# Decode attention and a Mish layer on one core: w2's seventh rows on partitions 0 to 63, last values in 3/4 and 1/4, o turned ahead of w2's products

## The chip, the cores and the metric

The kernel runs on one core of one Trainium2 chip. The time is device time in microseconds (us) of one execution. The kernel before was run three times: 1311.62, 1311.73 and 1311.91 us, median 1311.73. Only its own profile and trace were at hand when the prediction was written.

## What is computed

One decode step of a layer that adds attention over a long cache and a dense layer with Mish to its input. Cut to what matters:

```python
x: (8, 1, 512)                       # 8 sequences, one new token each
xn  = layernorm(x)
# A: attention, 32 query heads over 8 key heads, cache of 8192 positions, 128 per head
q   = (xn @ wq) by heads;  k, v = caches (8, 8, 8192, 128), each used by 4 query heads
p   = softmax(q . k * 128**-0.5);  o = p @ v;  A = o @ wo          # wo: (4096, 512)
# B: the dense layer
h   = xn @ w1 + b1                                                 # w1: (512, 1792)
act = h * tanh(softplus(h));       B = act @ w2                    # w2: (1792, 512)
return x + A + B
```

All is float32. The two caches hold 268 MB each, and every byte of them is read once.

## The kernel before

The caches are read as 64 blocks of 8 MB: for each of 16 packs p (a pair of key heads and two sequences b = 0, 1) one block of k and one of v per sequence, with 64 KB on each of the 128 partitions. Three buffers in SBUF take them in turn. `kva` ("a") takes w1, one block of k and then the blocks of v; `kvb` ("b") takes the blocks of k, at the end the block of v of the last pack's first sequence and after it w2; `kvw` ("w") takes wq and wo, 2 MB at a time.

All loads stand in one list (`queue`). `plan` (L114) appends one load per part; a part is a share of the columns of all 128 partitions. `pump` (L103) takes loads from the front while their buffer is free and issues them on SyncE (SP), and `release` (L110) gives a buffer up when the products that read it have been written down. On the chip SP waits for those products, by columns: a part's load is issued when PE has read the columns that it overwrites. The order of the loads is thus fixed, and SP is the only engine that issues them; ScalarE (ACT) issues two small ones at the start, x and b1. PE, VectorE (DVE) and GpSimd run in the order in which the code is written, which L710 to L727 make a rule.

The main loop (L651) computes for each pack the scores (`scores`, L348, products c on PE), the row maximum, exponents on ACT, their transposes and sums on DVE (`weights`, L423), and, one pack behind, the products with v (`values`, L454: 32 matmuls for a block, four column groups in each round, two trace records for a matmul). `gather` (L468) picks and adds the parts of a sequence's products (one DVE instruction and three more), `merge` (L484) sums them over partition groups with one matmul and scales them into `oT`. After the four packs of a pair of heads `turn` (L498) turns o so that it can be multiplied with wo: one DVE copy of the identity into `tid`, four matmuls, and four copies of 32 partitions into `oW`, for the last pair alternately on DVE and ACT.

`mish` (L567) runs once near the start: h for 1792 columns as four groups of 448 on four groups of partitions, some 14 DVE instructions, and a transpose into `aT`, the operand of w2's products. w2 lies in `kvb` as seven rows of 1024 numbers on each partition. `down(lo, hi)` (L620) multiplies rows lo to hi: 2 x 4 matmuls a row.

The end of the kernel (L687 to L708), in PE's order: the values of the last pack's first sequence (from `kvb`), its sums and merge, `add_up` (x and the earlier outputs), the values of the second sequence in two halves (from `kva`, loaded in two parts), w2's first four rows, the merge, the turn, half of wo's products, w2's fifth and sixth row, the other half of wo's, w2's seventh row. DVE copies the sum and SP stores it. The loads of this end, in SP's order:

```python
    plan_v(PACKS - 1, 0, "b")
    plan_v(PACKS - 1, 1, "a", ((0, 1 / 2), (1 / 2, 1)))
    W2_PARTS = ((0, 4), (4, 6), (6, 7))
    for k, (lo, hi) in enumerate(W2_PARTS):
        plan("w2", "b", w2, ((lo / W2R, hi / W2R),))
        if k < 2:
            plan_wo(PAIRS - 1, ((k / 2, (k + 1) / 2),))
```

Of the kernel before, what the change touches and what calls it, by code (L numbers as in the profile page):

```python
# [8 lines left out]
F32 = mybir.dt.float32  # L9
# [4 lines left out]
P = 128  # L14
B = 8
D = 512
# [49 lines left out]
OR = 4  # L66
W1R = 2 * CC * P // P
W2R = G * FT // 2 * FP // P
FAR = 1e38


@with_exitstack
def kernel(
# [40 lines left out]
    def plan(what, at, blocks, parts=((0, 1),), lo=0):  # L114

        rows = rows_of(blocks)
        n = rows.shape[1]
        t = place[at][:, lo : lo + n]

        def load(cols):  # L120
            nc.sync.dma_start(t[:, cols], rows[:, cols])
            return t

        for first, end in parts:
            cols = slice(int(first * n), int(end * n))
            queue.append((what, at, lambda cols=cols: load(cols)))


# [28 lines left out]
    def plan_wo(i, parts=((0, 1),)):  # L157
        plan(("wo", i), "w", wo[i * 4 : i * 4 + 4], parts)


    plan_wq(0)
    plan("w1", "a", w1)
# [10 lines left out]
            if p > 0:  # L173
                plan_v(p - 1, b, "a")
    plan_v(PACKS - 1, 0, "b")
    plan_v(PACKS - 1, 1, "a", ((0, 1 / 2), (1 / 2, 1)))
    W2_PARTS = ((0, 4), (4, 6), (6, 7))
    for k, (lo, hi) in enumerate(W2_PARTS):
        plan("w2", "b", w2, ((lo / W2R, hi / W2R),))
        if k < 2:  # L180
# [36 lines left out]


    xnT = const.tile([P, QR, 2, Q], F32, name="xnT")
    aT = const.tile([P, 2 * W2R, Q], F32, name="aT")  # L220
    xw = aT.rearrange("p j q -> p (j q)")[:, : W1R * 2 * B]
    xw = xw.rearrange("p (r t b) -> p r t b", r=W1R, t=2)

    def setup():
        make_identity(nc, ident)
        nc.gpsimd.memset(ones, 1.0)
        nc.vector.memset(xnT, 0.0)
        nc.vector.memset(H, 0.0)

        st = const.tile([B, 8], F32, name="st")  # L230

        scratch = pt.rearrange("p b c m t e h -> p (b c m t e h)")
        xc, sq = scratch[:B, :D], scratch[:B, D : 2 * D]
        nc.vector.reduce_sum(st[:, 0:1], x_sb, axis=AX.X)
        nc.vector.tensor_scalar_mul(st[:, 1:2], st[:, 0:1], 1.0 / D)
        nc.vector.tensor_scalar(xc, x_sb, st[:, 1:2], None, op0=ALU.subtract)
        nc.vector.tensor_mul(sq, xc, xc)
        nc.vector.reduce_sum(st[:, 2:3], sq, axis=AX.X)
        nc.vector.tensor_scalar(
            st[:, 3:4], st[:, 2:3], 1.0 / D, EPS, op0=ALU.mult, op1=ALU.add  # L240
        )
        nc.scalar.activation(st[:, 4:5], st[:, 3:4], AF.Sqrt)
        nc.vector.reciprocal(st[:, 5:6], st[:, 4:5])

        nc.vector.tensor_mul(st[:, 6:7], st[:, 5:6], st[:, 5:6])
        nc.vector.tensor_mul(st[:, 7:8], st[:, 6:7], st[:, 3:4])
        nc.vector.tensor_scalar(st[:, 6:7], st[:, 7:8], -0.5, 1.5, op0=ALU.mult, op1=ALU.add)
        nc.vector.tensor_mul(st[:, 4:5], st[:, 6:7], st[:, 5:6])
        nc.vector.tensor_scalar(xc, xc, st[:, 4:5], None, op0=ALU.mult)
        for r in range(QR):  # L250
            nc.tensor.transpose(M[:, r * B : (r + 1) * B], xc[:, r::QR], ident[:B, :B])
        nc.vector.tensor_copy(
            xnT[:, :, :, :B],
            M[:, : QR * B]
            .rearrange("p (r o b) -> p r o b", r=QR, o=1)
            .to_broadcast([P, QR, 2, B]),
        )
# [24 lines left out]
        nc.vector.memset(csel, 0.0)  # L282
        for c in range(2):
            rows = slice(HE * c, HE * (c + 1))
            for b in range(PB):
                nc.vector.tensor_copy(
                    csel[rows, b, :, b], ident[rows, rows].rearrange("p (u h) -> p u h", u=KN)
                )
        return wide
# [205 lines left out]
                RT.pop(p).rearrange("p b e h -> p (e h) b"),  # L495
            )

    def turn(i):  # L498


        to = oW[i] = work.tile([P, OR, 2, B], F32, name="oW")

        tid = work.tile([P, HT * KINDS * P], F32, name="e", bufs=1)[:, : OR * P]
        tid = tid.rearrange("p (r g i) -> p r g i", r=OR, g=G)
        nc.vector.tensor_copy(
            tid, ident.rearrange("p (i r o) -> p r o i", r=OR, o=1).to_broadcast([P, OR, G, Q])
        )
        o = oT.pop(i).rearrange("p n h b -> p (n h b)")
        cols = 2 * REP * B
        for r in range(OR):  # L510
            nc.tensor.matmul(
                M[:, 256 + r * cols : 256 + (r + 1) * cols],
                tid[:, r].rearrange("p g i -> p (g i)"),
                o,
                start=True,
                stop=True,
            )
        m = M[:, 256 : 256 + OR * cols].rearrange("p (r j q) -> p j r q", r=OR, j=G)
        for j in range(G):
            rows = slice(Q * j, Q * (j + 1))  # L520
            dst = to[rows].rearrange("p r h b -> p r (h b)")
            if i == PAIRS - 1 and j % 2:
                nc.scalar.copy(dst, m[rows, j])
            else:
                nc.vector.tensor_copy(dst, m[rows, j])
# [41 lines left out]
    def mish(w1_sb):  # L567


        hp = H[:, :FG]  # L570
        for g in range(G):
            nc.tensor.matmul(
                hp[Q * g : Q * g + B, :], gsel[:, g, :], b1_sb, start=True, stop=False
            )
        for r in range(W1R):
            for g in range(G):
                at = r * F // 2 + g % 2 * FG
                nc.tensor.matmul(  # L578
                    hp[Q * g : Q * g + B, :],
                    xw[:, r, g // 2, :],  # L580
                    w1_sb[:, at : at + FG],
                    start=False,
                    stop=(r == W1R - 1),
                )

        scratch = work.tile([P, HT * KINDS * P], F32, name="e", bufs=1)
        h, a, z, z2 = (scratch[:, i * 512 : i * 512 + FG] for i in range(4))
        nc.vector.tensor_copy(h, hp)


        nc.vector.scalar_tensor_tensor(a, h, -1.0, h, op0=ALU.mult, op1=ALU.max)
# [2 lines left out]
        m = a  # L594
        nc.vector.tensor_single_scalar(m, h, 0.0, op=ALU.is_gt)

        one = acc[:, :FG]
        nc.vector.tensor_scalar(one, z2, -1.0, 1.0, op0=ALU.mult, op1=ALU.add)
        nc.vector.tensor_mul(one, one, m)
        t1 = m  # L600
# [6 lines left out]
        nc.vector.tensor_mul(t1, t2, z)  # L607
        act = one
        half = FG // 2
        for e in range(2):  # L610
            nc.vector.tensor_mul(
                act.rearrange("p (i a e l) -> p e a l i", a=2, e=2, i=W2R)[:, e],
                h[:, half * e : half * (e + 1)].rearrange("p (a l i) -> p a l i", a=2, i=W2R),
                t1[:, half * e : half * (e + 1)].rearrange("p (a l i) -> p a l i", a=2, i=W2R),
            )
# [4 lines left out]
    def down(lo, hi, w):  # L620

        for j in range(2 * lo, 2 * hi):
            for g in range(G):
# [3 lines left out]
                    aT[:, j, :B],  # L627
                    w[:, at : at + P],
                    start=False,
                    stop=(j == 2 * W2R - 1),  # L630
                )


# [17 lines left out]
    for p in range(PACKS):  # L651
        for b in range(PB):
# [7 lines left out]
            if b == 0 and p > 0:  # L660
                sums(p - 1, lsel.pop(p - 1))
                if p > 1 and (p - 1) % NP == 0:
                    turn((p - 1) // NP - 1)
            rows(b)
            if b == 1:
                maximum(p)
# [19 lines left out]

    p = PACKS - 1  # L687
    merges()
    values(0, landed["v", p, 0])
    gather(p, 0)  # L690
    release(("v", p, 0))
    sums(p, lsel.pop(p))
    merge(p, 0)
    add_up()
    values(1, landed["v", p, 1], 0, ROUNDS // 2)
    values(1, landed["v", p, 1], ROUNDS // 2)
    gather(p, 1)
    w2_sb, wo_sb = landed["w2"], landed["wo", PAIRS - 1]
    down(*W2_PARTS[0], w2_sb)
    merge(p, 1)  # L700
    turn(PAIRS - 1)
    last_outputs(0, OR // 2, wo_sb)
    down(*W2_PARTS[1], w2_sb)
    last_outputs(OR // 2, OR, wo_sb)
# [61 lines left out]
```

## Time and profile before

| | us |
|---|---|
| median of three runs | 1311.73 |
| the profiled execution, its own time | 1311.59 |
| its span, first to last instruction | 1309.8 |
| DVE reads the finished sum, from the span's start | 1307.02 |
| PE busy in the span | 858.9 |
| DVE busy in the span | 384.7 |
| ACT busy in the span | 111.6 |

The profile is of one execution, and its times count from the start of the span; the 1.8 us that the execution's own time is longer lie around the span. A row of the chain of waits has the start, the length in us, and the engine and line or the transfer that the end of the kernel hung on. A row of the timeline has the start, the length, the engine, the line, the operation, output and input, and in brackets the idle time before it and what ended it. PEld is the load of a matmul's weights, which runs beside PE. A row of the DMA issues has the transfer, the issuing engine's queue (SPq, ACTq), how many, the size of each and the median time from issue to landing. Queue q1 is SP's, q10 is ACT's. A row of the windows has the window, its length, the busy time and records of each engine, the granted clock of PE as a share of full speed, the share of the 16 DMA engines that was busy, and GB/s.

### The profile page before, as it was taken

How to read it: one execution, taken by the hardware profiler on the slowest of the kernel's cores; microseconds unless marked ns; L12 is line 12 of the kernel's file. 1: busy time of each engine (PE TensorE's matmuls, PEld its weight loads, DVE VectorE, ACT ScalarE, POOL GpSimd, SP SyncE). 2: the span in 40 equal slices, each digit the busy share in tenths (PEclk: the TensorE clock that was granted, in tenths of full speed). 3: DMA queues.
4: the chain of work that ended last, by engine and by line, in shares of the span. 5: the costliest groups of instructions: out<-in, count | busy, mean ns of one | idle time of the engine just before them, and what ended most of it. 6: DMA issues, size and time to landing. Idle time of an engine off the chain costs nothing.

```text
span 1309.8 us, 10688 instructions
## 1 busy us (share of the span) xinstructions
PE 858.9 (66%) x4764; PEld 278.7 (21%) x4764; DVE 384.7 (29%) x590; ACT 111.6 (9%) x294; POOL 4.8 (0%) x10
## 2 busy tenths in 40 slices
PE   4786556856567765677566686665775666766567
PEld 1221112212112221122211222111221221222113
DVE  6150505205051230521405032052320505114051
ACT  1020101001010100101101010010100101011010
POOL 1000000000000000000000000000000000000000
PEclk9897889887799788898878897878987888878888
DMA  9999999999999999999999999999999999999997
GB/s 404 443 421 441 429 437 428 434 439 425 438 429 439 429 437 425 441 423 445 419 440 423 418 448 425 441 425 439 427 435 426 429 437 423 443 427 435 435 424 334
DMA packets 11446, 561.76 MB, mean 429 GB/s; under 512 B 1276, under 2 KB 1408, under 8 KB 1544
## 3 DMA queue, kind: packets, MB, share of 16 engines
q1 hardware_dynamic: 11376, 561.06, 99.3%
q8 instruction: 37, 0.61, 0.2%
q10 hardware_dynamic: 24, 0.02, 0.0%
q14 instruction: 9, 0.07, 0.0%
HBM read 561.01 MB, written 0.07 MB: 428 GB/s over the span
## 4 chain that ended last, share of the span: by engine, by line
DMA 60%; PE 35%; DVE 4%; issue 0%; ACT 0%; ACTq 0%; DVEq 0%
DMA kvb<-in_kT 56%; PE c L353 31%; DMA kva<-in_kT 2%; PE o L460 2%; DMA kvb<-in_w 2%; DVE raw L412 1%; DVE pt L430 1%; PE h L578 0%; PE h L312 0%; DVE nm L379 0%; PE s L365 0%; PE h L625 0%; DVE raw L421 0%; DVE os L473 0%; PE h L559 0%
## 5 line engine op out<-in xcount | busy, mean ns | idle before, releaser
L353 PE MATMUL c<-kvb,qT 128*64 128x512 f32 x1984 | 497.7, 665 | 348.4 <-DMA kvb<-in_kT 325.8
L353 PEld LDWEIGHTS c<-kvb,qT 128*64 128x64 f32 x1984 | 160.8, 154 | 685.3 <-issue 381.8
L460 PE MATMUL o<-kva,pt 128*32 128x512 f32 x1984 | 234.3, 626 | 25.5 <-DMA kva<-in_v 25.5
L379 DVE TENSOR_REDUCE nm<-s 128x1 f32<-128x1024 f32 x16 | 19.6, 1225 | 462.5 <-PE s L365 462.5
L412 DVE STREAM_TRANSPOSE raw<-e 128x2048 f32<-128x2048 f32 x32 | 116.0, 3627 | 14.4 <-ACT e L404 12.7
L360 ACT COPY sc<-c 128x512 f32<-128x512 f32 x32 | 18.7, 585 | 1001.3 <-PE c L353 1001.3
L460 PEld LDWEIGHTS o<-kva,pt 128*32 128x32 f32 x1984 | 64.5, 115 | 185.2 <-issue 144.1
L404 ACT ACTIVATE e<-s,nms 128x512 f32<-128x512 f32 x128 | 86.2, 685 | 126.2 <-DVE nms L393 66.8
L492 DVE TENSOR_TENSOR oT<-m,r 128x16 f32<-128x16 f32 x16 | 2.8, 175 | 233.6 <-PE m L488 233.6
L471 DVE TENSOR_SCALAR os<-o,isel 128x128 f32<-128x128 f32 x32 | 11.2, 350 | 152.0 <-PE o L460 152.0
L430 DVE TENSOR_TENSOR pt<-raw 64x256 f32<-64x256 f32 x128 | 53.6, 419 | 2.0
L365 PE MATMUL s<-sc,csel 64*128 64x512 f32 x128 | 36.1, 641 | 8.1 <-ACT sc L360 8.1
L421 DVE TENSOR_TENSOR raw<-raw 128x1024 f32<-128x1024 f32 x32 | 39.2, 1226 | 1.1
L340 DVE TENSOR_TENSOR qT<-qc,bsel 128x1024 f32<-128x1024 f32 x32 | 37.7, 1219 | 0.0
L473 DVE SCALAR_TENSOR_TENSOR os<-o,isel,os 128x128 f32<-128x128 f32 x96 | 33.7, 351 | 3.4
L404 ACT ACTIVATION_READ_ACCUMULATOR e<-s,nms 128x1 f32 x128 | 26.0, 203 | 0.0
L380 PE MATMUL m<-ident,nm 128*1 128x128 f32 x16 | 4.3, 270 | 21.2 <-DVE nm L379 21.2
L312 PE MATMUL h<-kvw,xnT 128*64 128x512 f32 x64 | 16.4, 660 | 0.0
L488 PEld LDWEIGHTS m<-hsel,os 128*128 128x128 f32 x64 | 9.5, 188 | 27.9 <-issue 23.7
L460 PE MATMUL o<-kvb,pt 128*32 128x512 f32 x64 | 9.5, 758 | 8.5 <-DVE oT L492 8.5
L353 PE MATMUL c<-kva,qT 128*64 128x512 f32 x64 | 14.0, 593 | 1.4 <-DMA kva<-in_kT 1.4
L323 DVE TENSOR_SCALAR e<-h 128x512 f32<-128x512 f32 x16 | 9.9, 683 | 16.1 <-PE h L312 16.1
(98 smaller groups left out, 170.8 us busy)
## 6 DMA issues: line engine op xcount, KB each, us to landing
kvw<-in_wq SPq DMA_DIRECT2D x4, 2048.0 KB, 31.1
kva<-in_v SPq DMA_DIRECT2D x2, 4096.0 KB, 23.5
kvw<-in_wo SPq DMA_DIRECT2D x3, 2048.0 KB, 30.4
kva<-in_w SPq DMA_DIRECT2D x1, 3584.0 KB, 16.0
kvb<-in_w SPq DMA_DIRECT2D x1, 2048.0 KB, 20.5
kvw<-in_wo SPq DMA_DIRECT2D x2, 1024.0 KB, 24.4
kvb<-in_w SPq DMA_DIRECT2D x1, 1024.0 KB, 24.1
kvb<-in_w SPq DMA_DIRECT2D x1, 512.0 KB, 26.9
```

The costliest lines, as they stand in the source:

```text
L312: nc.tensor.matmul(H[HE * e : HE * (e + 1), :], xnT[:, r].rearrange("p g q -> p (g q)"), w[:, r * BW + e * D : r * BW + (e + 1) * D], star ...
L340: nc.vector.tensor_mul(qT[:, b], qc[:, k * PB + b] .rearrange("p r (o h) -> p r o h", o=1) .to_broadcast([P, KR, KN, REP]), bsel.rearrange ...
L353: nc.tensor.matmul(C[b][HE * c : HE * (c + 1), :], t[:, r], k[:, r * BW + c * 512 : r * BW + (c + 1) * 512], start=(r == order[0]), stop=( ...
L360: nc.scalar.copy(sc, C[b])
L365: nc.tensor.matmul(S[:, c * 512 : (c + 1) * 512], csel[HE * c : HE * (c + 1), b].rearrange("p u b h -> p (u b h)"), sc[HE * c : HE * (c + ...
L379: nc.vector.tensor_reduce(nm, S, axis=AX.X, op=ALU.max, negate=True)
L404: nc.scalar.activation(ex[:, :, s, :], S[:, c * 512 : (c + 1) * 512].rearrange("p (t f) -> p t f", t=HT), AF.Exp, bias=NMS[p][:, s : s + 1 ...
L412: nc.vector.transpose(raw.rearrange("p (m t r) -> p t m r", m=TW, t=HT), ex.rearrange("p t s (q m) -> p t m (s q)", m=TW),)
L421: nc.vector.tensor_add(raw[:, :, :n], raw[:, :, :n], raw[:, :, n:])
L430: nc.vector.tensor_add(pt[rows, b, c].rearrange("p m t e h -> p (m t) e h")[:, :, e], raw[rows, :, at : at + REP], raw[rows, :, V8 + at : ...
L460: nc.tensor.matmul(O[b][Q * c : Q * (c + 1), :], pt[:, b, j % 2, j // 2].rearrange("p t e h -> p (t e h)"), vt[:, W4 * DH * j : W4 * DH * ...
L473: nc.vector.scalar_tensor_tensor(os, O[b][:, DH * i : DH * (i + 1)], isel[:, i : i + 1], os, op0=ALU.mult, op1=ALU.add,)
```

## The change

It has four parts, three of them at the end of the kernel.

- The load of w2's seventh rows. Before, it was the last load of SP's queue, 4 KB for each of 128 partitions. Now `plan_last_w2` issues it on ACT, ahead of the rest of w2 in the list: eight transfers, transfer k to the partitions k, k + 8, ... k + 56 of the first 64. Each of these partitions takes two rows, its own seventh and that of the partition 64 above it. On SP then stand w2's first four rows, half of wo, the fifth row, the other half of wo, the sixth row.
- `mish` computes the seventh rows' part of act a second time in the arrangement that this needs: 2 + 16 more matmuls of 64 columns into the PSUM buffer O[0], vectors of 512 columns for 448, one DVE copy, one DVE product and one memset more.
- The values of the last sequence are loaded and multiplied in 3/4 and 1/4. Between the two stands `last_down`, the 16 matmuls of the seventh rows, on 64 partitions.
- `turn` is split: the copy of the identity (`turning`) goes to the start of the end, and the merge and the turn stand ahead of `down` of the first four rows.

```diff
+    def plan_last_w2():
+        rows = w2.rearrange("j p f -> (j p) f").rearrange(
+            "(x e k i) f -> k i e x f", x=2, e=8, i=W2R
+        )
+        t = place["b"][:, (W2R - 1) * BW : W2X * BW].rearrange("p (x f) -> p x f", x=2)
+
+        def load():
+            for k in range(HE // 8):
+                nc.scalar.dma_start(t[k : HE : HE // 8], rows[k, W2R - 1])
+            return place["b"]
+
+        queue.append(("w2", "b", load))
...
-    plan_v(PACKS - 1, 1, "a", ((0, 1 / 2), (1 / 2, 1)))
-    W2_PARTS = ((0, 4), (4, 6), (6, 7))
+    plan_v(PACKS - 1, 1, "a", ((0, 3 / 4), (3 / 4, 1)))
+    plan_last_w2()
+    W2_PARTS = ((0, 4), (4, 5), (5, 6))
...
+        for g in range(2):
+                at = r * F // 2 + g * FG
+                nc.tensor.matmul(
+                    hx[Q * g : Q * g + B, :],
+                    xw[:, r, 1, :],
+                    w1_sb[:, at + W2R - 1 : at + FG : W2R],
...
+    def last_down(w):
+        for j in range(2 * W2R - 2, 2 * W2X):
+            for g in range(G):
+                at = j * D + g * P
+                nc.tensor.matmul(
+                    H[Q * g : Q * g + B, :P],
+                    aT[:HE, j, :B],
+                    w[:HE, at : at + P],
+                    start=False,
+                    stop=False,
+                )
...
     merges()
+    tid = turning()
     values(0, landed["v", p, 0])
...
     add_up()
-    values(1, landed["v", p, 1], 0, ROUNDS // 2)
-    values(1, landed["v", p, 1], ROUNDS // 2)
+    values(1, landed["v", p, 1], 0, ROUNDS * 3 // 4)
+    w2_sb, wo_sb = place["b"], landed["wo", PAIRS - 1]
+    last_down(w2_sb)
+    values(1, landed["v", p, 1], ROUNDS * 3 // 4)
     gather(p, 1)
-    w2_sb, wo_sb = landed["w2"], landed["wo", PAIRS - 1]
+    merge(p, 1)
+    turn(PAIRS - 1, tid)
     down(*W2_PARTS[0], w2_sb)
-    merge(p, 1)
-    turn(PAIRS - 1)
     last_outputs(0, OR // 2, wo_sb)
     down(*W2_PARTS[1], w2_sb)
     last_outputs(OR // 2, OR, wo_sb)
```

More of the change, by code (lines that the diff above doesn't have):

```diff
@@ L68 @@
 W2R = G * FT // 2 * FP // P
+W2X = W2R + 1
+XG = FG // W2R
 FAR = 1e38
@@ L124, in plan @@
         for first, end in parts:
-            cols = slice(int(first * n), int(end * n))
+            cols = slice(round(first * n), round(end * n))
             queue.append((what, at, lambda cols=cols: load(cols)))
@@ L219 @@
     xnT = const.tile([P, QR, 2, Q], F32, name="xnT")
-    aT = const.tile([P, 2 * W2R, Q], F32, name="aT")
+    aT = const.tile([P, 2 * W2X, Q], F32, name="aT")
     xw = aT.rearrange("p j q -> p (j q)")[:, : W1R * 2 * B]
@@ L228, in setup @@
         nc.vector.memset(H, 0.0)
+        nc.vector.memset(O[0][:, :XG], 0.0)
         st = const.tile([B, 8], F32, name="st")
@@ L496, in merge, with turning @@
             )
-    def turn(i):
-        to = oW[i] = work.tile([P, OR, 2, B], F32, name="oW")
+    def turning():
         tid = work.tile([P, HT * KINDS * P], F32, name="e", bufs=1)[:, : OR * P]
@@ L507, in turn @@
         )
+        return tid
+    def turn(i, tid):
+        to = oW[i] = work.tile([P, OR, 2, B], F32, name="oW")
         o = oT.pop(i).rearrange("p n h b -> p (n h b)")
@@ L570, in mish @@
         hp = H[:, :FG]
+        hx = O[0][:, :XG]
         for g in range(G):
@@ L573, in mish @@
                 hp[Q * g : Q * g + B, :], gsel[:, g, :], b1_sb, start=True, stop=False
+            )
+        for g in range(2):
+            nc.tensor.matmul(
+                hx[Q * g : Q * g + B, :],
+                gsel[:, 2 + g, :],
+                b1_sb[:, W2R - 1 :: W2R],
+                start=True,
+                stop=False,
             )
@@ L584, in mish @@
                 )
+            for g in range(2):
+                at = r * F // 2 + g * FG
+                nc.tensor.matmul(
+                    hx[Q * g : Q * g + B, :],
+                    xw[:, r, 1, :],
+                    w1_sb[:, at + W2R - 1 : at + FG : W2R],
+                    start=False,
+                    stop=(r == W1R - 1),
+                )
         scratch = work.tile([P, HT * KINDS * P], F32, name="e", bufs=1)
-        h, a, z, z2 = (scratch[:, i * 512 : i * 512 + FG] for i in range(4))
-        nc.vector.tensor_copy(h, hp)
+        n = FG + XG
+        h, a, z, z2 = (scratch[:, i * 512 : i * 512 + n] for i in range(4))
+        nc.vector.tensor_copy(h[:, :FG], hp)
+        nc.vector.tensor_copy(h[:, FG:], hx)
         nc.vector.scalar_tensor_tensor(a, h, -1.0, h, op0=ALU.mult, op1=ALU.max)
@@ L595, in mish @@
         nc.vector.tensor_single_scalar(m, h, 0.0, op=ALU.is_gt)
-        one = acc[:, :FG]
+        one = acc[:, :n]
         nc.vector.tensor_scalar(one, z2, -1.0, 1.0, op0=ALU.mult, op1=ALU.add)
@@ L609, in mish @@
         half = FG // 2
+        nc.vector.tensor_mul(
+            act[:, FG:].rearrange("p (a e l) -> p a e l", a=2, e=2),
+            h[:, FG:].rearrange("p (e a l) -> p a e l", a=2, e=2),
+            t1[:, FG:].rearrange("p (e a l) -> p a e l", a=2, e=2),
+        )
         for e in range(2):
             nc.vector.tensor_mul(
-                act.rearrange("p (i a e l) -> p e a l i", a=2, e=2, i=W2R)[:, e],
+                act[:, :FG].rearrange("p (i a e l) -> p e a l i", a=2, e=2, i=W2R)[:, e],
                 h[:, half * e : half * (e + 1)].rearrange("p (a l i) -> p a l i", a=2, i=W2R),
@@ L629, in down @@
                     start=False,
-                    stop=(j == 2 * W2R - 1),
+                    stop=(j == 2 * W2R - 3),
+                )
+    def last_down(w):
+        for j in range(2 * W2R - 2, 2 * W2X):
+            for g in range(G):
+                at = j * D + g * P
+                nc.tensor.matmul(
+                    H[Q * g : Q * g + B, :P],
+                    aT[:HE, j, :B],
+                    w[:HE, at : at + P],
+                    start=False,
+                    stop=False,
                 )
@@ L662 @@
                 if p > 1 and (p - 1) % NP == 0:
-                    turn((p - 1) // NP - 1)
+                    turn((p - 1) // NP - 1, turning())
             rows(b)
```

## The prediction, made before the changed kernel ran

> **What bounds the kernel now.** I read the page first, its engine shares and its queues, then the chain of waits and the instructions of the last 50 us, because every edit but one in the mish block lies there.
>
> ```profile
> span 1309.8 us, 10688 instructions
> DMA  9999999999999999999999999999999999999997
> q1 hardware_dynamic: 11376, 561.06, 99.3%
> q10 hardware_dynamic: 24, 0.02, 0.0%
> ```
>
> SP's queue (q1) keeps the DMA engines busy in every slice but the last: the kernel is a 561 MB stream, and only what happens while the stream ends can move the time by more than a fraction. The chain of waits over the end:
>
> ```profile
> 1272.95 3.67 PE o L460 x16
> 1276.64 20.51 DMA kvb<-in_w
> 1297.20 1.93 PE h L625 x64
> 1299.13 0.33 PE m L488 x2
> 1299.48 0.18 DVE oT L492
> 1299.66 0.53 DVE e L505
> 1300.23 1.12 PE m L511 x8
> 1301.38 0.22 DVE oW L525
> ...
> 1302.11 0.21 ACT oW L523
> 1302.37 1.90 PE h L559 x32
> 1304.27 1.37 PE h L625 x32
> 1305.63 0.87 PE h L559 x32
> 1306.51 0.49 PE h L625 x16
> 1307.02 0.29 DVE acc L707
> ```
>
> From 1297.20 on the end is set by computing: w2's first rows have landed, and PE, DVE and ACT pass o along one after the other until DVE reads the sum at 1307.02. But the stream is close behind. The last issues with their times to landing, and two windows of the end (columns: window, us, busy of PE, PEld, DVE, ACT, POOL, clock, DMA share, GB/s):
>
> ```profile
> kva<-in_v SPq DMA_DIRECT2D x2, 4096.0 KB, 23.5
> kvb<-in_w SPq DMA_DIRECT2D x1, 2048.0 KB, 20.5
> kvb<-in_w SPq DMA_DIRECT2D x1, 512.0 KB, 26.9
> 1259.08 3.76 SPq L121 DMA_DIRECT2D kva<-in_v  x2
> 1279.04 0.44 SPq L121 DMA_DIRECT2D kvb<-in_w  x1
> 1298.00:1301.50 3.50, 2.55 (x54) 2.10 (x42) 0.82 (x3) 0.00 (x0) 0.00 (x0) 1.00 0.98 407
> 1301.50:1305.40 3.90, 3.03 (x64) 2.28 (x68) 0.31 (x2) 0.41 (x2) 0.00 (x0) 0.56 0.44 181
> ```
>
> w2's last 512 KB land at 1279.04 + 26.9 = 1305.9, about 0.6 us ahead of their use at 1306.51. And the engines don't end together: at 0.98 until 1301.5, then 0.44 for 3.9 us. I read this as about half of the sixteen done near 1302 and the others some 2.6 us later (0.44 x 3.9 = 1.7 us of work that all sixteen could have shared).
>
> **The change, part by part.** *Mish.* 18 more matmuls, 36 records, and vectors of 512 columns for 448.
>
> ```profile
> 20.18 6.20 PE L578 MATMUL h<-kva,aT 128*8 128x448 f32 x64
> 26.44 0.33 SPq L121 DMA_DIRECT2D kva<-in_kT  x1
> 1.63 0.42 SPq L121 DMA_DIRECT2D kvb<-in_kT  x1
> kvb<-in_kT SPq DMA_DIRECT2D x1, 35.9
> ```
>
> At most 36 x 6.20/64 = 3.5 us on PE. What waits for it is SP's issue of the second k block at 26.44; the first one still moves until 1.63 + 35.9 = 37.5, so 11 us of stream cover it, less some 3 us for engines that end early. DVE's additions (a seventh more columns) come before the first maximum and hide behind the same stream. I take 0; without the cover it would be 3.5 us.
>
> *Last values.* The first piece grows from 4 to 6 MB.
>
> ```profile
> 1272.95 9.47 PE L460 MATMUL o<-kvb,pt 128*32 128x512 f32 x64 [8.47 <-DVE oT L492]
> 1284.84 5.23 PE L460 MATMUL o<-kva,pt 128*32 128x512 f32 x32
> 1292.30 3.64 PE L460 MATMUL o<-kva,pt 128*32 128x512 f32 x32 [2.23 <-DMA kva<-in_v]
> 1284.80:1288.20 3.40, 3.36 (x20) 0.92 (x24) 0.52 0.98 419
> 1296.01 0.35 DVE L471 TENSOR_SCALAR os<-o,isel 128x128 f32<-128x128 f32 x1 [11.84 <-PE o L460]
> 1296.40 1.12 DVE L473 SCALAR_TENSOR_TENSOR os<-o,isel,os 128x128 f32<-128x128 f32 x3
> ```
>
> The first half landed at 1259.08 + 23.5 = 1282.6, the second at 1292.3: 4 MB in 9.7 us, so three quarters land at 1287.4. Then 48 records: 20 in 3.4 us at the clock of 0.52 that the row shows after a lull, 28 at 3.64/32 = 0.114 us, 6.6 in all: PE is done at 1294.0. The last quarter is 1.82 us instead of 3.64. Shifted PE work ahead of the last landing saves nothing by itself, as PE was waiting there (2.23 us).
>
> *Turn.* The copy of the identity (0.53) leaves the chain for a place at 1272.8, where DVE's next step waits for the 9.47 us of values on kvb. The merge and turn no longer stand behind w2's 64 records, and the four copies of oW (1301.38 to 1302.33) hide behind those 1.93 us. Together about 1.5 us off the chain of computing, if PE can start it in time.
>
> *w2's seventh rows.* Removed: the row as last transfer of SP. Added: eight transfers on ACT's queue, each eight partitions of two 4 KB rows, issued when PE is through half of the values on kvb (32 records, 16 after w2's issue at 1276.64: about 1278.4). In PE's order their 16 matmuls stand between the third and the fourth quarter of the values and wait for all eight; behind them are queued the last quarter, the merge, the turn, everything to the end. So what matters is when they land. The trace has one transfer of this kind beside SP's stream, b1's four rows, issued on ACT at 1.37. Three windows of DMA packets, 3.3 to 5.8, 5.8 to 6.5, 6.5 to 7.1:
>
> ```profile
> 1.37 0.26 ACTq L135 DMA_DIRECT2D acc<-in_b  x1
> DMA packets 64, 1.05 MB, mean 419 GB/s; under 512 B 0, under 2 KB 0, under 8 KB 0
> ...
> DMA packets 21, 0.29 MB, mean 408 GB/s; under 512 B 0, under 2 KB 4, under 8 KB 4
> ...
> DMA packets 20, 0.26 MB, mean 437 GB/s; under 512 B 4, under 2 KB 4, under 8 KB 4
> ```
>
> Until 5.8 only SP's 16 KB packets move (64 in 2.5 us on 16 engines, 0.6 each). The four rows come in the next 0.7 us, and the four small packets, the completions, only in the window after: between a row and its own completion an engine put a packet of SP's. So ACT's packets get every second place. And q10's 24 packets are 8 + 4 rows and 8 + 4 completions: a transfer of eight partitions runs on eight engines, not sixteen. Each of the eight engines therefore has 8 x (2 rows + 1 completion) = 24 packets from ACT, each behind one packet of SP's. On a late engine, from 1279.4 (an issue takes 0.3 us and, I estimate, 0.7 to the first byte): five packets of the 48 KB kind are left (each 4.9 x 6/16 = 1.8 us; the first began at 1282.6 - 9.7 = 1272.9), then a completion, eight of 16 KB, a completion, eight of w2's first part, a completion: that is the 24th. So ACT's last completion on a late engine comes when w2's first part would have landed, 1276.64 + 20.5 = 1297.1, plus ACT's own 64 KB there, 8 x 0.31 = 2.5 (2 MB in 4.9 us is 0.61 for 16 KB, 0.31 for 8): **1299.6**. On an early engine 2.6 less, 1297.0. I take the late one: eight engines out of sixteen, half of them late, hold at least one late one unless they are exactly the early half. From above: b1 waited 4.4 us from issue to row, some five packets of SP's instead of one; four more of 0.31 to 0.6 put the landing up to 2 us later, 1301.6.
>
> [...]
>
> *Waits of SP.* In the built program w2's first part now also waits for the completion of the 6 MB (the count is shared), wo's second half for the last quarter, the others for ACT's third to fifth transfer. At 1287.4 two more MB (4.9 us) stand in the queue, at 1292.3 the 2 MB of w2; at both times the early engines have 4.9 - 2.6 = 2.3 us left, more than the 1.0 of an issue. Cost 0, and up to 2 us on early engines alone if issue to first byte took b1's 4.4 us.
>
> *The end of the stream.* The eight engines carry 64 KB of the seventh rows instead of 32 (+1.2 us), the others none (-1.2). With a late one among the eight the last landing is 1305.9 + 1.2 = 1307.1; if they are the early half, 1304.7.
>
> *Sum.* From ACT's landing at 1299.6: last_down's 32 records 0.87, last quarter 1.82, gather 0.07 + 1.51, merge 0.06 + 0.33, oT 0.02 + 0.18, turn 0.05 + 1.12, w2's 64 records 1.93, then 0.87 + 0.49 + 0.87 + 0.49 for outputs and rows (each at the faster of its two rows) and 0.1 of gaps: 10.8, so DVE would read at 1310.4, 3.4 late. PE has then waited over 5 us from 1294.0, and the rows show clocks of 0.52 and 0.56 after lulls: one stretch of 3.4 us at half speed is 1.7 us of work (none: 0; two: 3.4). 1312.1, **5.1 us late**: span 1314.9, and with 1311.59 - 1309.8 = 1.8 around it 1316.7. The run profiled was 0.14 us under the median of 1311.73; I leave that out.
>
> **Rivals.** *ACT's transfers land in time* (a place for each transfer, not each row): the 8th place on a late engine falls after v's second 16 KB packet, near 1290. Then PE goes on at 1294.0 and has 10.8 us to go, 1304.8; the stream decides with 1307.1 + 0.5 (the last 16 records) = 1307.6: 0.6 late, 1312.3. For it: nothing else in the trace has eight transfers on ACT. Against it: b1. *The eight engines are the early half* and the transfers are in time: landing 1304.7, so both ends agree near 1305.2, 1.8 us sooner, 1309.8; the change would then have levelled the tail that the 0.44 window shows. This is the case on the other side. It decides if ACT's rows have landed by 1294.9 and the late engines are all among the eight without them; the windows show the two halves, not their numbers. *The transfers do gate PE, but only on early engines:* landing at 1297.0, 2.6 us less than forecast, 1314.1.
>
> **How the numbers follow.** Gated by a late engine 0.60; gated by early ones 0.10; in time with the stream deciding 0.16; in time and levelled 0.14. The forecast is the first, 1316.7, its own range 1315.0 (no slow stretch) to 1320.4 (landing 2 us later, and two stretches). About 0.2%, 2.6 us, is what a measurement of this kernel can tell from no change: 1309.1 to 1314.4. The first case is slower throughout; of the second, 0.3 us under the bound, half is; 0.65 together. Of the levelled case I give half to more than 2.6 us, 0.07. The rest, 0.28, is the same. The range, 1310.0 to 1319.8, leaves half of the levelled case and the top of the gated one outside.
>
> **What would show it.** Right: PE idle for some 5 us ahead of last_down's first product, with DMA kvb<-in_w as what ends it; the fourth quarter of the values near 1300.5; the last of ACT's eight transfers landing near 1299.6 and w2's last row near 1307; the copies of oW gone from the chain. Wrong: last_down right behind the 48 records; all engines ending together, without the 3.9 us at 0.44; DMA idle between 1287 and 1297, which would mean that SP's added waits cost something.

## The result and the profile after

The changed kernel takes 1323.13 us in the median of six runs (1322.07 to 1323.84), the kernel before beside it on the same chip 1311.88 (1311.62 to 1313.41): a ratio of 1.0083, 95% interval 1.0070 to 1.0096. It is slower, as forecast, but by 11.2 us instead of 5.0, and outside the range (up to 1319.8). The profiled execution took 1323.84, its span 1321.9.

The page of the changed kernel: span, queues.

```profile
span 1321.9 us, 10811 instructions
...
q1 hardware_dynamic: 11376, 560.53, 98.5%
...
q10 hardware_dynamic: 216, 0.55, 0.1%
```

ACT's queue q10 went from 24 packets to 216: 192 more, 24 for each of the eight transfers, as counted; that they lie on eight engines no row shows. The chain of waits over the end (start, us, what):

```profile
1273.20 6.34 PE o L478 x32
...
1279.56 0.71 ACTq L171
...
1280.31 10.27 DMA kvb<-in_w
...
1290.60 12.25 DMA kvb<-in_w
1302.85 0.20 issue
1303.04 1.89 PE h L685 x32
1304.94 3.61 PE o L478 x16
...
1311.00 1.97 PE m L532 x8
1312.97 3.43 PE h L672 x64
1316.40 0.87 PE h L580 x32
1317.28 0.44 PE h L672 x16
1317.71 0.87 PE h L580 x32
1318.59 0.49 PE h L672 x16
...
1319.10 0.29 DVE acc L769
```

The chain also shows what the prediction hadn't counted: ACT's eight issues don't follow one another at once. The transfer issued second, at 1280.31, lands at 1290.58, and the last issue follows at 1290.60; the seventh came at 1287.88. By 1290 64 of ACT's 192 packets had passed, of the 168 that were issued, so the queue didn't run dry on the whole, and no run shows a cost of these waits.

last_down in the timeline:

```profile
1303.04 1.89 PE L685 MATMUL h<-kvb,aT 64*8 64x128 f32 x32 [7.45 <-DMA kvb<-in_w]
```

The wait that I forecast is there: last_down (L685) starts when the last of ACT's transfers has landed, and all that follows stands behind it in PE's order. From the landing to DVE's read at 1319.10 every piece is computing. What is off is where the two parts of it end. The landing is 1302.85, not 1299.6 (3.25 us). From last_down's start to the read it is 16.06 us, not 10.8 + 1.7 = 12.5 (3.56). With 0.19 between landing and start that is the 7.0 us by which the span, 1321.9, is longer than the 1314.9 of the sum.

The tail's pieces have the lengths of half speed (the last quarter 3.61 us instead of 1.82, w2's 64 records 3.43 instead of 1.93). The windows of the changed kernel (columns as before: window, us, busy times, clock, DMA share, GB/s):

```profile
1284.00:1298.00 14.00, 8.03 (x58) 2.12 (x58) 0.64 (x3) 0.00 (x0) 0.00 (x0) 0.76 0.96 319
1299.10:1303.00 3.90, 0.00 (x0) 0.00 (x0) 0.00 (x0) 0.00 (x0) 0.00 (x0) 0.50 1.00 392
1303.00:1316.20 13.20, 11.26 (x122) 6.46 (x126) 2.01 (x7) 0.41 (x2) 0.00 (x0) 0.50 0.25 104
1316.20:1319.10 2.90, 2.82 (x104) 2.38 (x96) 0.01 (x1) 0.00 (x0) 0.00 (x0) 1.00 0.00 0
```

The clock is 0.50 from 1299.1 to 1303.0 while PE waits and stays there for another 13.2 us, in which PE is busy for 11.3. And between 1284 and 1298, while ACT's rows move, the engines are nearly as busy as before (0.96, 0.99 before) but carry only 319 GB/s. Before, in the same window:

```profile
1284.00:1298.00 14.00, 10.29 (x106) 3.59 (x110) 1.57 (x6) 0.00 (x0) 0.00 (x0) 0.88 0.99 421
```

That is (421 - 319) x 14 us = 1.4 MB less, 3.4 us of stream. No term of my sum had it: the same bytes were to pass at the same rate. An idle queue it is not, since the share stays at 0.96. The packets themselves became slower. The queues between 1290 and 1298 show it (packets, MB, the share of 16 engines' time that they took), first before, then after:

```profile
q1 hardware_dynamic: 334, 3.29, 97.9%
```

```profile
q1 hardware_dynamic: 160, 2.26, 83.9%
q10 hardware_dynamic: 112, 0.30, 14.1%
```

Before, SP's 3.29 MB took 0.979 x 16 x 8 = 125 us of engine time, 0.62 us for 16 KB; after, 2.26 MB took 107 us, 0.78 us for 16 KB. The prediction had 0.61.

### The profile page after: what moved, and what is told of

Same layout as the page of the kernel before. It is cut to its first block, busy times and chain, and to the rows that moved or that the text cites. A ratio compares the mean times of both kernels' runs of the same rounds, so it can differ in the third digit from the quotient of the medians.

```text
span 1321.9 us, 10811 instructions
## 1 busy us (share of the span) xinstructions
PE 889.8 (67%) x4816; PEld 286.6 (22%) x4816; DVE 386.4 (29%) x593; ACT 111.8 (8%) x294; POOL 4.8 (0%) x10
## 2 busy tenths in 40 slices
DMA packets 11638, 561.76 MB, mean 425 GB/s; under 512 B 1340, under 2 KB 1472, under 8 KB 1864
## 4 chain that ended last, share of the span: by engine, by line
DMA 56%; PE 38%; DVE 5%; issue 1%; ACT 0%; ACTq 0%; DVEq 0%
DMA kvb<-in_kT 43%; PE c L371 28%; DMA kva<-in_v 8%; PE o L478 6%; DMA kvb<-in_v 2%; DMA kva<-in_kT 2%; DMA kvb<-in_w 2%; DVE raw L430 1%; DVE pt L448 1%; PE s L383 1%; PE h L609 1%; DVE os L491 0%; PE m L532 0%; DVE raw L439 0%; PE h L330 0%
## 5 line engine op out<-in xcount | busy, mean ns | idle before, releaser
L478 PE MATMUL o<-kva,pt 128*32 128x512 f32 x1984 | 252.8, 667 | 24.9 <-DMA kva<-in_v 24.9
L489 DVE TENSOR_SCALAR os<-o,isel 128x128 f32<-128x128 f32 x32 | 11.2, 350 | 175.2 <-PE o L478 175.2
L383 PE MATMUL s<-sc,csel 64*128 64x512 f32 x128 | 39.0, 688 | 8.3 <-ACT sc L378 8.3
L506 PE MATMUL m<-hsel,os 128*128 128x8 f32 x64 | 12.6, 270 | 4.7 <-DVE os L491 3.3
```

The costliest lines, as they stand in the source:

```text
L383: nc.tensor.matmul(S[:, c * 512 : (c + 1) * 512], csel[HE * c : HE * (c + 1), b].rearrange("p u b h -> p (u b h)"), sc[HE * c : HE * (c + ...
L478: nc.tensor.matmul(O[b][Q * c : Q * (c + 1), :], pt[:, b, j % 2, j // 2].rearrange("p t e h -> p (t e h)"), vt[:, W4 * DH * j : W4 * DH * ...
L506: nc.tensor.matmul(M[:, at : at + 2 * REP], OS.pop((p, b)), hsel, start=True, stop=True)
```

## Experiments

Each time is a median, with the ratio to the kernel before run beside it on the same chip. That kernel took 1312.39 beside the wait alone, the two single transfers to 64 partitions and the first kind of filler; 1312.67 beside the second kind of filler, every fourth partition of the lower half, the row to 128 partitions and the turn alone; 1312.68 beside neighbours, both causes taken apart and the eight transfers on SP; 1312.04 beside the upper half.

**The wait alone.** last_down moved out of the way, everything else as changed:

```diff
-    last_down(w2_sb)
     values(1, landed["v", p, 1], ROUNDS * 3 // 4)
...
+    last_down(w2_sb)
     down(*W2_PARTS[2], w2_sb)
```

> The changed kernel with last_down moved from between the value quarters to just ahead of the sixth row's products. Theory 'gate' (PE, in its order, stands before last_down until ACT's last transfer has landed at 1302.85): nothing stands behind the wait any more, the values end near 1296.5, and the stream decides with its last landing at 1309.1: DVE reads near 1309.7, 2.7 us later than in the kernel before, 1314 to 1315. Rival 'stream' (the small rows on ACT's queue slow all transfers, and the wait is only their symptom): the landings bound it anyway, 1319 or more. If the clock after the wait was the larger part, the tail behind the values shows full clock and the time falls as under 'gate'.

Measured 1316.27 us, ratio 1.0029 (1.0018 to 1.0040). That lies between the 1314 to 1315 of 'gate' and the 1319 of 'stream'. 6.9 us of the loss are the wait and its clock; 3.9 are left though PE waits for ACT no more. I put most of them down to the stream (324 GB/s between 1284 and 1298); the runs on where the rows go test that.

**Fewer, larger transfers.** The eight transfers as one of 64 neighbouring partitions, on ACT, then on SP at the same place in the list:

```diff
-            for k in range(HE // 8):
-                nc.scalar.dma_start(t[k : HE : HE // 8], rows[k, W2R - 1])
+            nc.scalar.dma_start(t[:HE], rows[W2R - 1])
```

and for SP `nc.sync` in place of `nc.scalar`.

> The changed kernel with the seventh rows in one transfer of 64 partitions on ACT's queue in place of eight of eight. Theory 'gate by packets': on each of sixteen engines 8 rows and one completion, 9 places between SP's packets instead of 24 on eight engines; it lands by 1292, last_down does not wait (PE arrives at 1294.6), last landing 1306 to 1307: 1311 to 1313. Rival 'any transfer on ACT's queue beside SP's': it lands after 1297 as in the changed kernel, 1316 or more.

> The changed kernel with the seventh rows in one transfer of 64 partitions on SP's queue, at the same place of the list. Theory 'gate by packets': no alternation at all, it lands right behind the last values, near 1293.5, last_down starts by 1295 and the stream ends where it did in the kernel before, 1305.9: 1311 to 1311.8, no slower than before. Rival 'the order of PE or the second quarter costs': 1313 or more without ACT's transfers.

On ACT 1314.92, ratio 1.0020 (1.0011 to 1.0029), which was to be 1311 to 1313. PE doesn't wait there, as expected (last_down at 1297.69, right behind the 48 records), but the stream carries 326 GB/s between 1284 and 1298 and w2's last rows land at 1309.61. On SP 1320.13, ratio 1.0054 (1.0037 to 1.0071), which was to be 1311 to 1311.8. In SP's own queue nothing alternates, and yet the transfer kept PE waiting, and the stream carried less than with any of ACT's. The timeline of the one on SP, and its window:

```profile
1300.14 1.88 PE L684 MATMUL h<-kvb,aT 64*8 64x128 f32 x32 [3.83 <-DMA kvb<-in_w]
```

```profile
1284.00:1298.00 14.00, 8.74 (x60) 2.43 (x60) 1.57 (x5) 0.00 (x0) 0.00 (x0) 0.76 0.98 285
```

285 GB/s at a share of 0.98. So the queue alone isn't the cause, and where the rows go came under suspicion: these transfers write partitions 0 to 63 alone.

**The clock.** PE kept at work during the wait, by 32 products that nobody reads, first on one column group, then on the four in turn:

```diff
+    for j in range(FILL):
+        nc.tensor.matmul(
+            C[0][:32, :],
+            pt[:, 1, j % 2, j // 2 % 16].rearrange("p t e h -> p (t e h)"),
+            landed["v", p, 1][:, 512 * (j % 16) : 512 * (j % 16 + 1)],
...
     last_down(w2_sb)
```

and for the four groups `C[0][Q * (j % G) : Q * (j % G + 1), :]` as the output.

> The changed kernel with 32 matmuls of 128x32 by 128x512 into an idle PSUM buffer between the third quarter of the values and last_down; their result is not used. Theory 'clock' (after 7.45 us of waiting PE runs the tail at half clock for four stretches): PE is kept busy for most of the wait, last_down still starts near 1303, and the 16.06 us from there to DVE's read shrink to 11 to 12: 1318 to 1319.5. Rival (the tail is long for other reasons): 1322 to 1324, with the granted clock at 1.0 in the tail or not.

> The changed kernel with 32 more matmuls of 128x32 by 128x512 into the unused C[0] between the third quarter of the values and last_down, in the four column groups in turn as the values are: work that nobody reads, to keep PE from idling while it waits for ACT's transfers. Theory (half speed behind the wait is what made the tail 16.1 us long instead of 10.8 to 12.5): the 64 records take 7 to 8 us, end by 1303.5, last_down starts within 1 us of the changed kernel's 1303.0, the clock behind it is 1.00, the tail is some 12.4 us, and the time is 1319 to 1320.5. Rival (the tail is long for another reason, such as rows that still arrive): 1322.5 to 1324.

The first took 1339.62, ratio 1.0207 (1.0192 to 1.0222): one column group is no filler, its 64 records ran 27.45 us and became the wait themselves, while ACT's last packet had passed by 1301.9. Its tail still speaks for the clock: from last_down at 1322.66 to the read at 1335.08 it took 12.42 us instead of 16.06, the quarter 1.90 instead of 3.61. The second, 1321.96, ratio 1.0074 (1.0060 to 1.0087), missed its 1319 to 1320.5. Its chain says why:

```profile
1304.54 0.93 issue
1305.46 1.06 PE h L686 x32
1306.52 1.90 PE o L479 x16
...
1317.92 0.29 DVE acc L778
```

The tail is 1317.92 - 1305.46 = 12.46 us instead of 16.06, last_down 1.06 instead of 1.89, the quarter 1.90 instead of 3.61, with a granted clock of 0.98 from 1305.4 to 1311 where the changed kernel had 0.50: the clock is what stretched it. But in this execution last_down started at 1305.46, 2.4 us later than in the changed kernel's, and that took back part. Half of the delay was there from the start: ACT issues when PE is through half of the values on `kvb`, at 1280.78 instead of 1279.56. What delayed the rest stays open.

**Where the rows go.** The same eight transfers of eight partitions on ACT, the same bytes and places in the queues; transfer k now writes every fourth partition of one half of the 64, not every eighth of all, or eight neighbours, or every fourth of a half 64 partitions higher:

```diff
-                nc.scalar.dma_start(t[k : HE : HE // 8], rows[k, W2R - 1])
+                a, j = divmod(k, 4)
+                nc.scalar.dma_start(t[32 * a + j : 32 * a + 32 : 4], rows[a, j, W2R - 1])
...
+                nc.scalar.dma_start(t[8 * k : 8 * k + 8], rows[k, W2R - 1])
...
+                nc.scalar.dma_start(t[HE + 32 * a + j : HE + 32 * a + 32 : 4], rows[a, j, W2R - 1])
```

w2's rows are indexed to match, so that in the first two each partition takes the rows that belong to it. The kernel of the upper half leaves out part of the result: its products there lack the second of the two rows' operand. Its instructions, bytes and places in the queues are the same.

> The changed kernel, but transfer k on ACT goes to every fourth partition of one half of the 64 (32a + j, 32a + j + 4, ... 32a + j + 28) instead of every eighth of all 64. Still eight transfers of eight partitions, the same bytes, the same eight engines, the same 24 places between SP's packets. [...] Rival (places in the queues alone decide, wherever the rows go): as the changed kernel, 1322 to 1324, landing 1302.5 to 1303.5.

> The changed kernel with transfer k on ACT to eight neighbours, partitions 8k to 8k + 7, instead of every eighth. The same engines, bytes and places in the queues. [...] Rival (what helped with every fourth partition of a half was something else than the spread, such as the order of the rows in DRAM): 1319.5 to 1324.

> As with every fourth partition of a half (1320.0), but the rows go 64 partitions higher, to the same eight places in the upper half, and last_down reads them there; the products' operand on these partitions lacks the second of the two rows, so w2's seventh rows come out of this run in part only, with the same instructions, bytes, engines and places in the queues. [...]

Every fourth of the lower half: 1320.03 (1319.47 to 1320.97), ratio 1.0061 (1.0046 to 1.0077), 3.1 us under the changed kernel; I had put it at 1319 to 1320.5. Neighbours: 1324.66, ratio 1.0092 (1.0077 to 1.0108), just under the 1325 to 1332 that I had put it at and not told apart from the changed kernel's 1.0083. Every fourth of the upper half: 1324.10, ratio 1.0091 (1.0074 to 1.0107), 4.1 us above the lower half; I had put it at 1322 to 1326. The window of each, in this order:

```profile
1284.00:1298.00 14.00, 8.73 (x58) 2.19 (x58) 0.00 (x0) 0.00 (x0) 0.00 (x0) 0.76 0.96 403
```

```profile
1284.00:1298.00 14.00, 7.63 (x58) 2.05 (x58) 0.23 (x2) 0.00 (x0) 0.00 (x0) 0.76 0.94 314
```

```profile
1284.00:1298.00 14.00, 7.51 (x48) 1.78 (x48) 0.00 (x0) 0.00 (x0) 0.00 (x0) 0.76 0.97 312
```

The share is that of a busy stream in all three; only the first keeps the rate. Between 1290 and 1298 SP's 3.03 MB took 89.8% of the engines' time in it, 0.62 us for 16 KB as before. And its landing is close to where the prediction had put it:

```profile
1287.34 11.66 DMA kvb<-in_w
1299.00 1.24 issue
1300.24 1.74 PE h L688 x32
...
1314.34 0.29 DVE acc L772
```

The 1299.00 of the chain isn't the landing of ACT's last transfer: ACT's last packet lies between 1299.3 and 1299.55, and last_down starts some 0.7 us behind it, as it does in the changed kernel (last packet before 1302.35, start 1303.04). Read as the 1302.85 there, the landing is about 1300.0.

Between the lower and the upper half the loads differ in nothing but 64 partitions. So it isn't how a transfer's eight partitions are spread alone (every fourth kept the rate in the lower half, 403 GB/s, and not in the upper, 312; neighbours did no clear harm beyond every eighth), nor the place in the queue. What is shown is that the same transfers cost or don't cost by the partitions that they write.

Why this way of sharing out the lower half keeps the rate isn't shown. No row tells which engine writes which partition, and that this is what counts was my guess. That the upper half alone is slow is no rival for the changed kernel, whose rows go to the lower half; the same eight sets of partitions in another order weren't run.

**Both causes taken apart.** The better places and last_down moved, together:

> ACT's eight transfers to every fourth partition of one half of the 64, as in the run before with these places (1320.0), and last_down moved to just ahead of the sixth row's products, so that PE doesn't wait for them. Theory (what last_down's move alone left over, 1316.3 against 1312.4, is the slowed stream, and these places don't slow it): the last landing is near 1307.1 and DVE's read near 1307.6 to 1308.2, the time 1312.2 to 1313.5. Rival (the 3.9 us that were left come from the eight transfers' number, or from the doubled load of eight engines): 1315 to 1317 again.

1313.27, ratio 1.0006 (0.9996 to 1.0015): no difference from the kernel before can be told. With the runs above this makes a square:

| us | last_down between the values | last_down near the end |
|---|---|---|
| every eighth partition | 1323.13 | 1316.27 |
| every fourth of a half | 1320.03 | 1313.27 |

The places are worth 3.1 and 3.0 us, the wait with its clock 6.9 and 6.8, whichever of the two is changed first (by the ratios, which leave out the difference between chips, 2.9 and 3.0, 7.1 and 7.2). The two account for 9.9 us of the loss; what is left is 0.6 to 1.4, by which of the medians of the kernel before (1312.68, 1311.88) one takes, and the medians themselves differ by as much.

**SP's queue with good places.** The seventh row as one transfer on SP to all 128 partitions (its products by `down(W2R - 1, W2R, w2_sb)` where last_down stood), and the eight transfers to every fourth partition of a half issued by SP:

```diff
-    plan_last_w2()
+    plan("w2", "b", w2, (((W2R - 1) / W2R, 1),))
...
-                nc.scalar.dma_start(t[32 * a + j : 32 * a + 32 : 4], rows[a, j, W2R - 1])
+                nc.sync.dma_start(t[32 * a + j : 32 * a + 32 : 4], rows[a, j, W2R - 1])
```

> The changed kernel, but the seventh row is one transfer on SP to all 128 partitions (4 KB each), at the same place in SP's list as the one transfer to 64 partitions that I tried, ahead of w2's first part; its 8 products stand where last_down stood. Theory (a transfer to partitions 0 to 63 alone is slow and slows the stream; one to 128 isn't): the row lands by 1294, PE isn't kept waiting by it, the stream ends near 1306, and the time is 1311.0 to 1312.5, 8 us less than with 64 partitions (1320.1). Rival (any transfer put ahead of w2's first part, behind the values, lands after 1299 and gates PE): 1319 to 1321.

> The eight transfers to every fourth partition of a half, now on SP's queue at the same place in the list, ahead of w2's first part. In one queue nothing alternates; the rows come behind v's last quarter. [...]

To 128 partitions: 1311.57, ratio 0.9994 (0.9984 to 1.0003), 8.6 us less than to 64 (1320.13), with the rest of the change (mish's additions, 3/4 and 1/4, the turn ahead) still in it. Its timeline has the row's products right behind the 48 records, without a wait, and its window the old rate:

```profile
1287.49 6.79 PE L478 MATMUL o<-kva,pt 128*32 128x512 f32 x48 [3.03 <-DMA kva<-in_v]
1294.10 0.61 PE L672 MATMUL h<-kvb,aT 128*8 128x128 f32 x16
1294.54 1.89 PE L478 MATMUL o<-kva,pt 128*32 128x512 f32 x16
```

```profile
1284.00:1298.00 14.00, 9.39 (x90) 2.65 (x89) 1.39 (x4) 0.00 (x0) 0.00 (x0) 0.88 0.96 407
```

Eight transfers on SP: 1315.07, ratio 1.0020 (1.0010 to 1.0029). PE doesn't wait for the rows (last_down at 1295.08), but the time missed its 1311.5 to 1313.5, for a reason of another kind. The windows of this run:

```profile
1290.00:1292.00 2.00, 2.00 (x16) 0.58 (x12) 0.00 (x0) 0.00 (x0) 0.00 (x0) 0.50 0.28 111
1292.00:1294.00 2.00, 2.00 (x20) 0.48 (x16) 0.00 (x0) 0.00 (x0) 0.00 (x0) 0.96 0.17 53
```

From 1290 to 1294 the engines are mostly idle. SP's timeline and its waits (what it waited for, us in all, times, longest):

```profile
1279.44 13.57 SPq L172 DMA_DIRECT2D kvb<-in_w  x8
```

```profile
SPq L172 <- DMA kva<-in_v: 7.8, 2, 4.2
```

The eight issues take 13.57 us, of which 7.8 are waits for v to land: I read it as with w2's first part in the prediction, that some of the eight share a completion count with them (the seventh is issued at 1287.48, the eighth at 1292.34), and while SP waits, w2 isn't queued. This is the price that the prediction named for SP's waits if the cover is gone.

**The turn alone,** on the kernel before: `turning()` at the start of the end, merge and turn ahead of w2's first four rows.

> The kernel before with one part of the change alone: the copy of the identity at the start of the end, and merge and turn ahead of w2's first four rows. Theory (1.5 us off the chain of computing, then the stream decides): DVE's last read of the sum falls from 1307.0 to about 0.5 us behind the last landing of w2 at 1305.9, so 1306.4 to 1306.6 and 0.4 to 0.6 us less in all, 1311.1 to 1311.4 beside 1311.7. Rival (the chain of computing doesn't get shorter, as the 64 records of w2 had filled PE's wait for o): no difference.

1312.23, ratio 1.0003 (0.9994 to 1.0011): no difference; the 0.4 to 0.6 us expected aren't seen. In its profile the stream decided, w2's last row landing at 1306.51 and DVE reading at 1307.24; whether the chain of computing became shorter by 1.5 us can't be read from it, as its values ran partly at half speed.

No version beat the kernel before beyond what the runs tell apart; the one to 128 partitions comes nearest.

## Why the prediction was right in direction and wrong in size

- *That ACT's transfers gate PE, and on a late engine:* the gate is right. last_down waited 7.45 us for them, and moving it away returned 6.9. A landing near 1300 and not near 1297 fits a late engine, but no row names the engine.
- *One place of ACT's for each row and completion, 24 per engine:* the time of the landing fits, though no row shows the turns one by one. With the rows on every fourth partition of the lower half the landing was about 1300.0, where the sum had 1299.6; by whole transfers it would have been near 1290. From ACT's first packet to its last (1283.10 to 1299.55) SP had 514 packets, some 32 on each of 16 engines, beside 192 of ACT's. That all eight transfers run on the same eight engines, 24 packets on each, no run shows: what the counts show is eight packets under 512 B for each of these transfers (1276 before, 1340 after) and sixteen for the one to 128 partitions (1292).
- *The landing at 1299.6:* wrong for the kernel as changed, by 3.25 us. The step that failed is the price of a packet: 0.61 us for 16 KB and 0.31 for 8, taken from the kernel before, where every load goes to all 128 partitions. With ACT's rows beside it SP's 16 KB took 0.78 us, and 0.62 again when the rows went to every fourth partition of the lower half. The start was off as well, if less: ACT's first packet passed at 1283.4, 3.9 us after its issue, where the sum had 1.0 (x's first packet in the kernel before passed at 1.70, 0.97 after its issue, when SP's stream had not begun) and the upper bound b1's 4.4. The sum counted packets and not where the rows are written. My upper bound, 1301.6, was built from more places for SP's packets, and did not reach it either.
- *One stretch of 3.4 us at half speed, 1.7 us of work:* mis-sized, the second term that failed. (In the end of the kernel before the clock was 0.50 from 1284.7 to 1288.1 and from 1301.7 to 1305.2, 3.4 us each.) The tail lost 5.3 us (16.06 - 10.8) to it in the profiled execution, nearly four such stretches; with the better places, where the chain reads from 1300.24 to 1314.34, 14.1 and so 3.3, about the upper value that I had named; with PE kept busy 1.7. One stretch is what remained in that run, where PE waited 1.56 us for the rows.
- *The end of the stream at 1307.1, and in time 1312.3 (the first rival):* that price is approached only with the better places and last_down out of the way, 1313.27. As changed, the windows end about 2 us later, with a share of 0.83 at 1304 to 1306 and 0.30 at 1306 to 1308:

```profile
1304.00:1306.00 2.00, 2.00 (x28) 0.73 (x22) 0.00 (x0) 0.00 (x0) 0.00 (x0) 0.50 0.83 342
1306.00:1308.00 2.00, 2.00 (x12) 0.20 (x4) 0.00 (x0) 0.00 (x0) 0.00 (x0) 0.50 0.30 123
```

- *Levelled ends (the rival on the other side):* not seen. None of the runs that left the rows in time was faster than before beyond its interval.
- *Mish at 0:* right, though PE's part is larger than my 3.5: the second k block is issued at 31.41 instead of 26.44, PE's clock having fallen to 0.50 there (1.00 from 20 to 25 before). The cover named still stands: PE then waits 6.39 us for the first block, where it waited 11.33 before. A window, SP's issue and the first scores of the changed kernel:

```profile
20.00:25.00 5.00, 5.00 (x40) 1.39 (x36) 4.73 (x4) 0.00 (x0) 0.00 (x0) 0.50 0.97 419
```

```profile
31.41 0.33 SPq L123 DMA_DIRECT2D kva<-in_kT  x1
...
37.76 7.52 PE L371 MATMUL c<-kvb,qT 128*64 128x512 f32 x22 [6.39 <-DMA kvb<-in_kT]
```

- *SP's waits at 0:* right to within half a microsecond with the rows on ACT's queue (the share is 0.96 from 1284 to 1298, where it was 0.99, and 1.00 from 1299.1 to 1303); with the eight on SP's own queue they do cost.
- *The turn:* the copies of oW are gone from the chain, as said; alone it brings nothing that can be measured, since the stream ends at the same time.

## What to carry to other kernels

When a side transfer is put beside a full stream, ask not only which queue it uses but which partitions it writes: 512 KB to every eighth of the first 64 partitions cost the stream 3 us here, the same bytes to every fourth of a half of them, or over all 128, nothing that could be told. A product that waits for such a transfer belongs behind the work that doesn't depend on it, since PE paid for the wait twice here, in the wait (7.45 us) and in the slow clock after it (0.50 for 13.2 us). And price a stall with the clock that follows: 1.7 us was the least of it, 3.3 to 5.5 what came in the five runs that waited.

## What the runs showed of the hardware that was not expected

- The stream fell from 421 GB/s to between 285 and 329 with the engines almost as busy (shares of 0.94 to 0.98), through 0.5 MB written to 64 partitions in any way that was run but one.
- The clock stayed at 0.50 for 13.2 us behind the wait, though PE worked without a gap from 1303.04 to 1308.55 within it. It fell at 1299.1 and rose at 1316.2, 17.1 us later. That is five times 3.41; the other stretches at 0.50, in this kernel and in the kernel before, take 3.41, 6.83, 10.24 or 13.65 us. Of the last four of the five pieces only the last is busy from end to end:

```profile
1302.50:1305.92 3.42, 2.88 (x40) 1.52 (x44) 0.00 (x0) 0.00 (x0) 0.00 (x0) 0.50 0.92 380
1305.92:1309.33 3.41, 2.59 (x16) 0.20 (x4) 0.70 (x2) 0.00 (x0) 0.00 (x0) 0.50 0.20 82
1309.33:1312.74 3.41, 2.33 (x10) 2.24 (x10) 0.88 (x3) 0.00 (x0) 0.00 (x0) 0.50 0.00 0
1312.74:1316.16 3.42, 3.42 (x66) 2.47 (x69) 0.43 (x2) 0.41 (x2) 0.00 (x0) 0.50 0.02 5
```

  With every fourth partition of the lower half the clock was 0.50 from 1300.45 to 1303.86, one such piece, busy throughout, and rose at its end. I read from these two that the length of the slow tail depends in part on how the work falls into such pieces; no run sets that apart. From last_down to the read it took 14.10 us there, 14.36 with neighbours, 15.07 with the upper half, 16.06 in the changed kernel and 16.34 with the single transfer on SP.
- What an issue costs went by the shape of the transfer rather than by who issues it: the single transfer to 64 partitions took 0.71 us on ACT and 0.71 on SP, one to eight spread partitions 0.61 to 0.81 on ACT and 0.67 to 0.86 on SP, one to eight neighbours 0.28 to 0.32 on ACT.
- 64 records of the same product took 27.45 us on one column group (the chain of waits of the first run with fillers) and 7.04 on four in turn (the timeline of the second):

```profile
1295.21 27.45 PE c L760 x64
```

```profile
1296.86 7.04 PE L760 MATMUL c<-kva,pt 128*32 128x512 f32 x64
```
